# Rounding the cosine's multiple of 2π by an int32 output instead of by adding and taking off a large constant

## The chip, the cores and the metric

The kernel runs on one core of one Trainium2 chip. The metric is device microseconds (us) of one execution; the median of three runs of the kernel before is 973.51 us (972.93 to 973.61).

## The reference

The program is a linear attention followed by two feed-forward layers, all in float32. The change lies in the first feed-forward layer alone:

```python
def _moe_ref(x, w_in, w_out):
    h = x @ w_in            # 2304 tokens, 512 -> 2048
    g = h * np.cos(h)
    return (g @ w_out).astype(np.float32)

def _moe2_ref(x, w_in, w_out):
    h = x @ w_in
    r = np.maximum(h, 0.0)
    g = r * r
    return (g @ w_out).astype(np.float32)

x = _moe_ref(x=attention_output, ...)
return _moe2_ref(x=x, ...)
```

## The kernel before

**Stages.** The attention (lines 802 to 964) runs to about 190 us of the profiled execution, the first feed-forward layer from there to about 595 us, the second from there to the end. All products of the feed-forward layers are float32 results made of three matmuls each: every operand is split into a high part of reduced precision and the rest, and high·high, high·rest and rest·high are summed in PSUM.

**Blocks and chunks of the first layer.** `feed_forward` goes over five blocks of tokens (`BLOCKS`, line 290): blocks 0, 2, 3 and 4 have 512 tokens, block 1 has 256. In a block, step i (0 to 18) works on the 16 chunks of 128 hidden features. `G1` (line 308) multiplies the split input with the split weights of chunk i: 12 matmuls into one of four PSUM banks, `h`. `G2` (line 376) multiplies the finished g of chunk i−3 with the second weights: 12 matmuls into four accumulators. So TensorE is given G1 of chunk i and then G2 of chunk i−3 in each step; steps 16 to 18 hold G2 alone. The first matmul of a G2 needs the high part of g, the second already needs the rest of it.

**The elementwise chain of a chunk** is cut into seven parts in `part` (line 320), which stand in `elementwise` (line 350) in the order B1 of chunk i−1, A1 of chunk i, B2 of i−1, A2a of i, B3 of i−1, A2b of i, B4 of i−1. ScalarE (ACT) and VectorE (DVE) each do their own in that order:

- A1, ACT: line 329 writes h/2π plus 12582912 (1.5·2^23, so the addition rounds to a whole number) to t, line 330 takes the constant off again.
- A2a and A2b, DVE, lines 332 and 334: r = h − C1·t, then r = r − C2·t, with C1 + C2 = 2π.
- B1, ACT, lines 336 and 337: sin(r/2), then its square times 2.
- B2, DVE, line 339: t = (1 − r)·h, which is h·cos(h).
- B3, ACT, line 344: the high part of g. B4, DVE, line 347: the rest of g.

t and r are halves of a tile `tr` of which two exist; `h` has four banks, g two tiles.

**What stands between them.** In block 0 the weights of the first layer that are still missing are converted (`ticks`, with DVE doing the combining steps). In blocks 1 to 3 the weights of the second layer are prepared ahead (`ahead`, line 551, called by `converts`, line 744, at places fixed by a count of matmul columns): a load (line 474), two ACT steps (lines 239, 241), three DVE steps (260, 262, 269), one POOL step (264), POOL sums (504), and then pieces of the result are split (ACT line 524, DVE line 525) into staging areas and sent to DRAM by the SP queue (line 526). An ACT split has to wait until the DMA that last read its staging area has landed. Block 4 prepares nothing of this kind, only the last weights and the start of the second layer. SP issues its DMAs in program order.

The order of the first four chunks of block 0 is arranged together with the last attention units by a table of costs and places (`F_STEPS`, `arrange`); everything behind them is in the order in which the code is written.

Of the kernel before, what the change touches and what calls it, by code (L numbers as in the profile page):

```python
# [10 lines left out]
I32 = mybir.dt.int32  # L11
U32 = mybir.dt.uint32
ACTF = mybir.ActivationFunctionType
ALU = mybir.AluOpType
# [1 line left out]
PSUM = bass.MemoryType.PSUM  # L16

INV_2PI = 0.15915494309189535
ROUND = 12582912.0
C1 = 6.28125  # L20
C2 = 6.283185307179586 - C1
START_0 = 0
# [142 lines left out]
def attention_ffn_kernel(  # L165
# [11 lines left out]
    nc = tc.nc  # L177
# [12 lines left out]
    def f(t):  # L190
        return t.bitcast(F32)

    with tc.manual_schedule():
# [11 lines left out]
        def work(tag, shape, dtype=F32, name=None):  # L205

            return shared.tile(shape, dtype, tag=tag, name=name or tag, bufs=BUFS[tag])
# [15 lines left out]
        def w_load(n):  # L223
            part, c = order[n]
            s = w_slot(n + 1, I32, [P, KDM * P, 2], "raw")
            nc.sync.dma_start(
                out=s.rearrange("p f t -> p (f t)"), in_=(w_in1, w_out1)[part].bitcast(I32)[c * P:(c + 1) * P, :]
            )
            raw_t[0, n] = words_of(s.rearrange("p (a f) t -> p a (f t)", a=2))
# [43 lines left out]
        def w_split(layer, n, part):  # L273
            m = mag_t[layer, n]
            if part == 0:
                if layer == 0:
                    t = w_slot(n, F32R, [P, 2, KDM * P], "w")
                    weights[(0, *order[n])] = t
                else:
                    t = w_slot(12 + n[1], F32R, [P, 2, KDM * P], "w")  # L280
                    weights[1, 1, n[1]] = t
                nc.scalar.activation(out=t[:, 0], in_=m, func=ACTF.Copy)
            else:
                t = weights[(0, *order[n])] if layer == 0 else weights[1, 1, n[1]]
                engine = nc.gpsimd if layer == 0 and n < NEARLY - 1 else nc.vector
                engine.tensor_tensor(out=t[:, 1], in0=m, in1=f(t[:, 0]), op=ALU.subtract)
                mag_t.pop((layer, n))
# [6 lines left out]
        xs_t, h_t, g_t, tr_t, acc, early = {}, {}, {}, {}, [], set()  # L294

        def split_x(j, kk, part):
            _, o, n = BLOCKS[j]
            src = xbuf[:, kk, o:o + n]
            x = work(XS[kk][part], [P, n], F32R, "xs")
            if part == 0:  # L300
                nc.scalar.activation(out=x, in_=src, func=ACTF.Copy)
                xs_t[kk] = (x,)
            else:
                hi = xs_t[kk][0]
                nc.vector.tensor_tensor(out=x, in0=src, in1=f(hi), op=ALU.subtract)
                xs_t[kk] = (hi, x)
# [13 lines left out]
        def part(name, j, c):  # L320

            n = BLOCKS[j][2]
            if (name, j, c) in early:
                return
            if name == "A1":
                tr_t[c] = work("e", [P, 2, n], F32, "tr")
            t, r = tr_t[c][:, 0], tr_t[c][:, 1]
            if name == "A1":
                nc.scalar.activation(out=t, in_=h_t[c], func=ACTF.Copy, scale=INV_2PI, bias=ROUND)  # L329
                nc.scalar.activation(out=t, in_=t, func=ACTF.Copy, bias=-ROUND)  # L330
            elif name == "A2a":
                nc.vector.scalar_tensor_tensor(out=r, in0=t, scalar=-C1, in1=h_t[c], op0=ALU.mult, op1=ALU.add)  # L332
            elif name == "A2b":
                nc.vector.scalar_tensor_tensor(out=r, in0=t, scalar=-C2, in1=r, op0=ALU.mult, op1=ALU.add)  # L334
            elif name == "B1":
                nc.scalar.activation(out=r, in_=r, func=ACTF.Sin, scale=0.5)  # L336
                nc.scalar.activation(out=r, in_=r, func=ACTF.Square, scale=SQRT2)  # L337
            elif name == "B2":
                nc.vector.scalar_tensor_tensor(  # L339
                    out=t, in0=r, scalar=1.0, in1=h_t.pop(c), op0=ALU.subtract, op1=ALU.mult, reverse0=True  # L340
                )
            elif name == "B3":
                g_t[c] = g = work("kq1", [P, 2, n], F32R, "g")
                nc.scalar.activation(out=g[:, 0], in_=t, func=ACTF.Copy)  # L344
            else:
                g = g_t[c]
                nc.vector.tensor_tensor(out=g[:, 1], in0=t, in1=f(g[:, 0]), op=ALU.subtract)  # L347
                tr_t.pop(c)
# [781 lines left out]
```

## Time and profile before

| what | value |
|---|---|
| median of three runs | 973.51 us |
| profiled execution, its own time | 972.84 us |
| profiled execution, span | 971.1 us |
| TensorE matmul busy (PE) | 956.7 us, 99% |
| TensorE weight loads busy (PEld) | 823.8 us, 85% |
| VectorE busy | 662.6 us, 68% |
| ScalarE busy | 579.6 us, 60% |
| GpSimd busy | 168.8 us, 17% |
| granted TensorE clock, mean | 1.000 |

The span runs from the first instruction to the last; the execution's own time is 1.7 us longer. PE and PEld are two queues of the same engine: weight loads run beside the matmuls before them. The ends of matmuls are modelled, so PE's idle time is a lower bound for what the engine loses; a late weight load on PEld shows it more fully. An idle time is put down to what ended it.

### The profile page before, as it was taken

To read this page: it belongs to the slowest core of one execution; us is meant where nothing else is said; L and a number is where in the kernel's file an instruction comes from. 1 tells how busy PE (TensorE), PEld (TensorE's weight loads), DVE (VectorE), ACT (ScalarE), POOL (GpSimd) and SP (SyncE) were. 2 spreads that over 40 slices of the span, in tenths; PEclk is the share of its full clock that TensorE was granted. 3 is DMA by queue.
4 is the path that set the end of the run, shared out by engine and by line. 5 is a ranking of instruction groups with operands and counts; after the bars stand their busy time and mean duration, and the time that the engine had idled before them with its cause. 6 is when DMAs were issued, how large, how long until landed. Compare 5 with 4: busy or idle time off the path is not lost.

```text
span 971.1 us, 15675 instructions
## 1 busy us (share of the span) xinstructions
PE 956.7 (99%) x5865; PEld 823.8 (85%) x5865; DVE 662.6 (68%) x1137; ACT 579.6 (60%) x1133; POOL 168.8 (17%) x146
## 2 busy tenths in 40 slices
PE   8999999999999999999999999999999999999998
PEld 7888888788899887788788888889889898988887
DVE  6788897589957676775868656877673434844444
ACT  4988877688867667766867664455442223432233
POOL 1666764100002033113300001212000000000000
PEclk9999999999999999999999999999999999999999
DMA  7566542242021055325244315665554435544411
GB/s 255 169 209 221 182 149 69 67 168 77 1 88 44 24 181 176 98 77 197 110 149 136 102 34 178 192 201 188 184 165 128 127 105 191 163 130 129 111 43 65
DMA packets 52283, 128.27 MB, mean 132 GB/s; under 512 B 6384, under 2 KB 12144, under 8 KB 52208
## 3 DMA queue, kind: packets, MB, share of 16 engines
q1 hardware_dynamic: 52064, 127.21, 40.7%
q8 instruction: 46, 0.75, 0.3%
q14 instruction: 29, 0.24, 0.1%
q10 hardware_dynamic: 144, 0.07, 0.0%
HBM read 102.99 MB, written 24.19 MB: 131 GB/s over the span
## 4 chain that ended last, share of the span: by engine, by line
PE 52%; ACT 3%; DVE 2%; DMA 1%; issue 1%; POOL 0%; SPq 0%; ACTq 0%; DVEq 0%
PE acc L668 20%; PE m L613 18%; PE acc L387 8%; PE h L317 2%; PE h L316 2%; PE h L315 2%; DMA sp<-xbuf 1%; ACT tr L329 1%; DVE tr L332 0%; ACT tr L330 0%; DVE tr L334 0%; ACT tr L336 0%; ACT xbuf L524 0%; DVE g L347 0%; DVE xbuf L525 0%
## 5 line engine op out<-in xcount | busy, mean ns | idle before, releaser
L668 PE MATMUL acc<-w,g 128*128 128x512 f32 x864 | 226.0, 394 | 0.0
L387 PE MATMUL acc<-g,w 128*128 128x512 f32 (+1 forms) x960 | 212.2, 370 | 6.2 <-DVE g L347 5.9
L387 PEld LDWEIGHTS acc<-g,w 128*128 128x128 f32 x960 | 167.7, 188 | 40.7 <-DVE g L347 10.0
L668 PEld LDWEIGHTS acc<-w,g 128*128 128x128 f32 x864 | 159.7, 188 | 23.3
L613 PE MATMUL m<-xc,wc 128*128 128x384 f32 x864 | 173.7, 336 | 0.8 <-DVE t L636 0.8
L613 PEld LDWEIGHTS m<-xc,wc 128*128 128x128 f32 x864 | 154.5, 188 | 14.2 <-DVE t L636 1.3
L315 PE MATMUL h<-xs,w 128*128 128x512 f32 (+1 forms) x320 | 117.9, 369 | 0.0
L316 PE MATMUL h<-xs,w 128*128 128x512 f32 (+1 forms) x320 | 117.8, 368 | 0.0
L317 PE MATMUL h<-xs,w 128*128 128x512 f32 (+1 forms) x320 | 117.7, 368 | 0.0
L595 DVE TENSOR_TENSOR g<-t,g 128x384 fp32r<-128x384 f32 x96 | 53.6, 579 | 77.7 <-ACT g L594 77.6
L594 ACT ACTIVATE g<-t 128x384 fp32r<-128x384 f32 x96 | 47.3, 518 | 65.6 <-DVE t L627 65.3
L264 POOL TENSOR_TENSOR mag<-mag,raw 128x512 int32<-128x512 int32 x36 | 48.2, 1339 | 212.5 <-ACT tr L337 90.0
L332 DVE SCALAR_TENSOR_TENSOR tr<-tr,h 128x512 f32<-128x512 f32 (+1 forms) x80 | 50.7, 633 | 39.5 <-ACT tr L330 38.9
L339 DVE SCALAR_TENSOR_TENSOR tr<-tr,h 128x512 f32<-128x512 f32 (+1 forms) x80 | 50.5, 631 | 33.7 <-ACT tr L337 33.4
L315 PEld LDWEIGHTS h<-xs,w 128*128 128x128 f32 x320 | 60.3, 188 | 10.3 <-issue 0.2
L316 PEld LDWEIGHTS h<-xs,w 128*128 128x128 f32 x320 | 60.4, 189 | 10.0
L317 PEld LDWEIGHTS h<-xs,w 128*128 128x128 f32 x320 | 60.3, 189 | 9.9
L336 ACT ACTIVATE tr<-tr 128x512 f32<-128x512 f32 (+1 forms) x80 | 46.7, 584 | 31.5 <-DVE tr L334 30.9
L869 PEld LDWEIGHTS kv<-v,e 128*128 128x128 f32 x512 | 60.2, 192 | 3.2 <-issue 1.4
L869 PE MATMUL kv<-v,e 128*128 128x65 f32 x512 | 62.5, 275 | 0.2
L344 ACT ACTIVATE g<-tr 128x512 fp32r<-128x512 f32 (+1 forms) x80 | 46.3, 580 | 27.2 <-DVE tr L334 11.7
L850 DVE TENSOR_REDUCE m<-pj 128x4 f32<-128x512 f32 (+1 forms) x80 | 49.9, 623 | 18.0 <-PE pj L835 10.0
(93 smaller groups left out, 1393.5 us busy)
## 6 DMA issues: line engine op xcount, KB each, us to landing
wc<-sp SPq DMA_DIRECT2D x72, 512.0 KB
raw<-in_dram SPq DMA_DIRECT2D x48, 512.0 KB
xbuf<-in_dram SPq DMA_DIRECT2D x16, 512.0 KB
sp<-xbuf SPq DMA_DIRECT2D x15, 512.0 KB
kq<-in_dram SPq DMA_DIRECT2D x16, 384.0 KB
wc<-sp SPq DMA_DIRECT2D x24, 256.0 KB
v<-in_dram SPq DMA_DIRECT2D x16, 330.0 KB
dn<-db SPq DMA_DIRECT2D x32, 144.0 KB
```

What stands on the lines that cost most here:

```text
L264: soon(layer, n).tensor_tensor(out=halves(mi), in0=halves(mi), in1=word0, op=ALU.add)
L315: nc.tensor.matmul(out=hps, lhsT=ih[:, kk, :], rhs=xh, start=kk == 0, stop=False)
L316: nc.tensor.matmul(out=hps, lhsT=ih[:, kk, :], rhs=xl, start=False, stop=False)
L317: nc.tensor.matmul(out=hps, lhsT=il[:, kk, :], rhs=xh, start=False, stop=kk == KDM - 1)
L332: nc.vector.scalar_tensor_tensor(out=r, in0=t, scalar=-C1, in1=h_t[c], op0=ALU.mult, op1=ALU.add)
L339: nc.vector.scalar_tensor_tensor(out=t, in0=r, scalar=1.0, in1=h_t.pop(c), op0=ALU.subtract, op1=ALU.mult, reverse0=True)
L387: nc.tensor.matmul(out=acc[m][:, 0:n], lhsT=l, rhs=r, start=c == 0 and i == 0, stop=c == KFF - 1 and i == 2)
L595: nc.vector.tensor_tensor(out=g[:, 1], in0=t, in1=f(g[:, 0]), op=ALU.subtract)
L613: nc.tensor.matmul(out=m, lhsT=l[:, sl], rhs=r[:, q], start=start and q == 0 and n == 0, stop=q == 1 and n == 2, skip_group_check=True,)
L668: nc.tensor.matmul(out=acc[m], lhsT=g[:, l, sl], rhs=w[:, r], start=p == 0 and f_ == 0 and i == 0, stop=p == NP - 1 and f_ == 1 and i == 2,)
L850: nc.vector.tensor_reduce(out=m[:, 0:n], in_=pj[:, 0:n, :], axis=AX.X, op=ALU.max, apply_absolute_value=True)
L869: nc.tensor.matmul(out=acc[:, s, h, 0:D + 1], lhsT=e[:, t, s, :], rhs=v_t[u][:, t, h, 0:D + 1], start=t == 0 and h == 0 and s == 0, stop=F ...
```

## The change

In A1 the two activations become one. It multiplies h by 1/2π and writes the result as int32 into the words of t, so that the conversion rounds to a whole number; the addition of the large constant and the activation that takes it off (64 of 128x512 and 16 of 128x256 elements) are gone. A2a and A2b read t as int32 in place of float32. B2 writes t as float32 as before. No instruction stands at another place: on ACT 80 of 1036 rows of the program's order are left out, the order of the others and of all other engines is the same.

```diff
-ROUND = 12582912.0
...
             if name == "A1":
-                nc.scalar.activation(out=t, in_=h_t[c], func=ACTF.Copy, scale=INV_2PI, bias=ROUND)
-                nc.scalar.activation(out=t, in_=t, func=ACTF.Copy, bias=-ROUND)
+                nc.scalar.activation(out=t.bitcast(I32), in_=h_t[c], func=ACTF.Copy, scale=INV_2PI)
             elif name == "A2a":
-                nc.vector.scalar_tensor_tensor(out=r, in0=t, scalar=-C1, in1=h_t[c], op0=ALU.mult, op1=ALU.add)
+                nc.vector.scalar_tensor_tensor(out=r, in0=t.bitcast(I32), scalar=-C1, in1=h_t[c], op0=ALU.mult, op1=ALU.add)
             elif name == "A2b":
-                nc.vector.scalar_tensor_tensor(out=r, in0=t, scalar=-C2, in1=r, op0=ALU.mult, op1=ALU.add)
+                nc.vector.scalar_tensor_tensor(out=r, in0=t.bitcast(I32), scalar=-C2, in1=r, op0=ALU.mult, op1=ALU.add)
```

## Rows read from the trace of the kernel before

**Rows 1.** The page's busy times, and the span's stretch of block 0 (--windows view).

```profile
PE 956.7 (99%) x5865; PEld 823.8 (85%) x5865; DVE 662.6 (68%) x1137; ACT 579.6 (60%) x1133; POOL 168.8 (17%) x146
...
195.00:272.00 77.00, 77.00 (x341) 63.30 (x340) 71.56 (x124) 61.72 (x110) 2.88 (x2) 1.00 0.21 75
```

**Rows 2.** Groups by line and shape: busy us, mean ns, idle before and its releasers.

```profile
L387 PEld LDWEIGHTS acc<-g,w 128*128 128x128 f32 x960 | 167.7, 188 | 40.7 <-DVE g L347 10.0 <-ACT g L344 1.3
```

**Rows 3.** Waits of PEld in blocks 0, 1, 2, 3: us in total, times, longest.

```profile
PEld acc L387 <- DVE g L347: 0.6, 2, 0.3
...
PEld acc L387 <- DVE g L347: 1.8, 4, 0.7
...
PEld acc L387 <- DVE g L347: 5.5, 5, 1.3
...
PEld acc L387 <- DVE g L347: 2.2, 2, 1.3
```

**Rows 4.** Timeline of PEld in block 2, G2 of chunks 7 to 9: start, us.

```profile
368.88 0.19 PEld L387 LDWEIGHTS acc<-g,w 128*128 128x128 f32 x1
370.41 2.37 PEld L387 LDWEIGHTS acc<-g,w 128*128 128x128 f32 x11 [1.34 <-DVE g L347]
...
375.54 2.68 PEld L387 LDWEIGHTS acc<-g,w 128*128 128x128 f32 x12
...
380.98 2.68 PEld L387 LDWEIGHTS acc<-g,w 128*128 128x128 f32 x12
```

**Rows 5.** Timeline of ACT and DVE, block 3, one turn without preparation work.

```profile
418.41 0.63 ACT L336 ACTIVATE tr<-tr 128x512 f32<-128x512 f32 x1 [1.48 <-DVE tr L334]
...
419.62 0.58 ACT L329 ACTIVATE tr<-h 128x512 f32<-128x512 f32 x1
419.74 0.69 DVE L339 SCALAR_TENSOR_TENSOR tr<-tr,h 128x512 f32<-128x512 f32 x1 [1.36 <-ACT tr L337]
420.23 0.63 ACT L330 ACTIVATE tr<-tr 128x512 f32<-128x512 f32 x1
...
420.89 0.69 DVE L332 SCALAR_TENSOR_TENSOR tr<-tr,h 128x512 f32<-128x512 f32 x1 [0.46 <-ACT tr L330]
421.61 0.69 DVE L334 SCALAR_TENSOR_TENSOR tr<-tr 128x512 f32<-128x512 f32 x1
...
422.34 0.63 ACT L336 ACTIVATE tr<-tr 128x512 f32<-128x512 f32 x1 [0.96 <-DVE tr L334]
```

**Rows 6.** Groups by line and shape: the removed operation, and two with int32.

```profile
L330 ACT ACTIVATE tr<-tr 128x512 f32<-128x512 f32 x64 | 40.5, 632 | 2.0
...
L241 ACT ACTIVATE raw<-raw 128x512 int32<-128x512 uint32 x48 | 32.3, 673 | 1.0 <-DMA raw<-in_dram 1.0
...
L269 DVE SCALAR_TENSOR_TENSOR mag<-raw,mag 128x512 int32<-128x512 int32 x28 | 19.4, 692 | 1.0
...
L330 ACT ACTIVATE tr<-tr 128x256 f32<-128x256 f32 x16 | 6.7, 418 | 0.5
```

**Rows 7.** Timeline of block 3 around an ACT wait for a staging area.

```profile
429.14 0.66 ACT L239 ACTIVATE mag<-xbuf 128x512 f32<-128x512 f32 x1
...
432.48 1.31 POOL L264 TENSOR_TENSOR mag<-mag,xbuf 128x512 int32<-128x512 int32 x1 [16.21 <-ACT tr L329]
...
433.82 0.56 SPq L474 DMA_DIRECT2D xbuf<-in_dram  x1
...
434.46 1.06 SPq L526 DMA_DIRECT2D sp<-xbuf  x2
...
439.71 0.63 ACT L524 ACTIVATE xbuf<-xbuf 128x512 fp32r<-128x512 f32 x1 [5.52 <-DMA sp<-xbuf]
...
441.66 0.62 ACT L336 ACTIVATE tr<-tr 128x512 f32<-128x512 f32 x1
```

**Rows 8.** All waits of the span: us in total, times, longest.

```profile
ACT xbuf L524 <- DMA sp<-xbuf: 21.7, 4, 5.7
...
ACT tr L329 <- PE h L317: 14.6, 15, 2.3
```

## The prediction
> **What bounds the kernel now.** I read the busy times first: TensorE is at 99%, DVE at 68%, ACT at 60%, and in the stretch of block 0 the granted clock is 1.00, the upper of its two levels [rows 1]. So what an ACT step less can give is limited to the time in which TensorE waits for the chain that this step belongs to. The groups by line show that time: the weight loads of G2 stand idle 10.0 us for DVE's line 347, the rest of g, and 1.3 us for ACT's line 344, its high part [rows 2]. By blocks it is 0.6 us in block 0, 1.8 in block 1, 5.5 in block 2 and 2.2 in block 3; block 4, which prepares nothing, has none [rows 3].
>
> An idle weight load is not quite a late TensorE, since a load may run a little ahead of its matmul. In block 2, G2 of chunk 8 starts 6.66 us after G2 of chunk 7, and that of chunk 9 starts 5.44 us after that of chunk 8; between the first two lies an idle time of 1.34 us [rows 4]. So 1.34 us shown cost 1.22, nine tenths. Nine tenths of 11.3 us are 10.2; I use **10.0 us** as all that there is to gain.
>
> Why is line 347 late? One turn of the chain without preparation work takes 3.93 us, from line 336 at 418.41 to the next at 422.34, though in it DVE stands idle for 1.36 + 0.46 us and ACT for 0.96: they wait for one another [rows 5]. This is below the 5.44 us of a TensorE step, so the chain would keep up. But the preparation steps stand in the same two queues, and four times ACT waits 5 to 6 us for a staging area, 21.7 us in all [rows 8]. ACT is then far behind: only 15 of the 80 A1 steps wait for their matmuls [rows 8], in the others the matmuls were done before.
>
> **The change part by part.**
>
> *The activation removed.* It takes 632 ns at 512 columns and 418 at 256, with some 30 ns of idle time before it [rows 6]. Where ACT is what the chain goes through, 0.66 us go (0.45 in block 1). In the undisturbed turn less goes: line 332 starts at 420.89, just behind line 330, but without that step it must still wait for line 339, which ends at 419.74 + 0.69 = 420.43 [rows 5]. So it starts at about 420.46, **0.43 us** earlier, and the turn takes 3.50 us. DVE's line 339 is what is late next.
>
> Beside the row stands a rule. For an activation with constant scale and bias the Trainium skill (ScalarE: Activation LUTs, What ACT_TABLE_LOAD costs) states 186 ns plus 0.833 ns per element of a row, with 93 ns of overlap between neighbours: 520 ns for 512. By it the first chunk of a block would gain 0.52 in place of 0.66 us and my sum would come out about 0.15 us higher; I go by the row.
>
> *The int32 output.* No row shows a PSUM source with an int32 output. The nearest is line 241, which writes int32 in 673 ns, against 580 for line 329 [rows 5, 6]; so between nothing and 0.09 us more. I take nothing: in the undisturbed turn it lies beside line 339 anyway, with about 0.2 us of cover (line 329 ends at 420.20, line 339 at 420.43) [rows 5].
>
> *The int32 operand of lines 332 and 334.* Line 269 on the same engine, with the same operation form, reads two int32 tiles in 692 ns, though with bit operations; line 332 takes 690 with float32 [rows 5, 6]. I take nothing. The far end is the POOL row of an int32 addition of the same shape, 1.31 us [rows 7], 0.62 more for each; that makes a rival below.
>
> *What the removal does to each stall.* At the start of a block the gain is 0.66 us at chunk 0 and 0.43 more with each chunk, 1.95 at chunk 3. A wait for a staging area comes in between: does it keep its place? The DMA that ACT waits for at 439.71 was issued at 434.46, right behind a load (433.82) that waited for POOL's line 264 (432.48 to 433.79), whose input goes back to ACT's own line 239 at 429.14 [rows 7]. So the whole detour starts in the ACT queue and moves forward with it; only the turn that lies inside the detour saves nothing.
>
> - Block 3: the first stall costs under 0.9 us (2.2 less the longest, 1.3) [rows 3] and has 1.95 against it; both together, with the wait for line 344, cost about 2.1, with two more chunks by then, 2.8. Both go.
> - Block 2: at chunk 7 seven chunks have gained some 2.9 us (0.66, then 0.43 each, a little less where ACT reaches TensorE and has to wait for it) against 1.2. At chunk 10 it is 4.1 against 2.6 so far. At the end, where G2 follows G2 every 2.7 us, chunk 13 has 4.5 against 4.1, chunk 14 has 4.8 against 5.3. **0.5 us stay.**
> - Block 1: the first stall, under 0.7 us, has at least 0.45 against it; the three of the tail, 1.1 us, have a dozen chunks behind them. I leave 0.1.
> - Block 0: two stalls of 0.3 us at the tail; one chunk's 0.43 to 0.66 covers them.
>
> **The sum.** 10.0 − 0.6 = 9.4 us. Nothing else follows TensorE's clock or changes its matmuls. The profiled execution took 972.84 us, so 963.4 against it; it stands 0.67 us under the median 973.51, and against the median the forecast is **964.1 us**.
>
> **The rivals.**
>
> *The waits for the staging areas keep their place* (faster, but by half). If loads and spills land when the DMA queues let them and not when ACT asks, the four stalls that follow such a wait stay: twice 1.34 in block 2, 2.2 in block 3 [rows 3, 4], 4.7 us with nine tenths and the little that line 344 adds. 10.0 − 0.6 − 4.7 = 4.7 us, so 968.8. For it speaks the size of these waits, up to 5.7 us [rows 8]; against it the chain of rows 7, in which nothing before line 239 sets the date.
>
> *No change, 973.5.* Either the int32 output takes as long as both steps (0.58 + 0.63), against the row of line 241, or TensorE is bound by its own work. The Trainium skill (Perfetto Trace Analysis, Identifying the Most-Contended Engine) has one look for the engine with the highest occupancy, for TensorE by the weight loads' share, and better that one first; ACT's 60% against 85% would make this change worth nothing. The rows speak against it for this stretch: the 85% is a mean, and the idle loads name their cause.
>
> *DVE becomes the bound* (slower). If an int32 operand in arithmetic takes 0.62 us more on lines 332 and 334, DVE gets 16 × 1.24 = 19.8 us more in block 0, where it is busy 71.56 of 77.00 us already [rows 1]. 5.4 us are free, so TensorE waits 14 us there, more than all the gain of the other blocks; with no gain elsewhere it is 973.5 + 14 = 987.5. The point from which DVE decides is 5.4 / 32, about 0.17 us more for each of the two. Line 269 speaks against it.
>
> **How the numbers follow.** A measurement of this kernel can tell about 0.2%, 1.9 us, from no change. The forecast, with its own range 962.6 to 966, has a chance of 0.66; the staging rival, or something between, up to 969, has 0.20; no change 0.06; slower 0.05; and 0.03 that the start of the second layer or the whole 11.3 us shown come on top. The range takes the first two, 962.4 to 968.9, and leaves out 0.14. Faster 0.89, same 0.06, slower 0.05.
>
> **What the profile would show.** Right: line 330 is missing; line 332 waits for line 339 on its own engine and no longer for ACT; a clean turn takes 3.5 us; the idle time of G2's weight loads for DVE's line 347 falls from 10.0 us to about 0.5, left at the tail of block 2; lines 332 and 334 keep 0.69 us. The four waits for staging areas are still there, as long or longer, but earlier in the block. Wrong: the stalls behind these waits are still of 1 us (second case), or lines 332 and 334 have grown (slower case), or the new line of A1 takes over 0.8 us.

## The result, and the profile after

The changed kernel takes 963.0 us (median of five, 962.58 to 963.75) against 973.53 (median of five runs on the same chip). The ratio is 0.9893, 95% interval 0.9882 to 0.9904: between 9.3 and 11.5 us less, 10.5 by the medians. The forecast was 964.1 us, within 962.4 to 968.9.

On the page of the changed kernel, TensorE is still at 99%, and ACT has lost 42.7 us of busy time (579.6 in [rows 1]):

```profile
PE 953.5 (99%) x5865; PEld 824.9 (86%) x5865; DVE 657.4 (68%) x1137; ACT 536.9 (56%) x1053; POOL 169.0 (18%) x146
```

So of 42.7 us taken off ACT a quarter came back as time. The groups by line and shape answer to [rows 2, 6]; line numbers are lower by one or two than before (A1 is 328, A2a 330, A2b 332, B1 334 and 335, B2 337, B3 342, B4 345, G2 385):

```profile
L385 PEld LDWEIGHTS acc<-g,w 128*128 128x128 f32 x960 | 168.0, 189 | 30.5 <-DVE g L345 0.6
...
L332 DVE SCALAR_TENSOR_TENSOR tr<-tr 128x512 f32<-128x512 int32 x64 | 44.9, 701 | 1.9
...
L330 DVE SCALAR_TENSOR_TENSOR tr<-tr,h 128x512 f32<-128x512 int32 x64 | 43.6, 681 | 13.9 <-ACT tr L328 13.4
...
L328 ACT ACTIVATE tr<-h 128x512 int32<-128x512 f32 x64 | 37.5, 587 | 18.9 <-PE h L316 17.2 <-DVE g L345 1.5
```

The first row is the result: the weight loads of G2 wait 0.6 us for the rest of g where they waited 10.0, and no longer for its high part. The others show that the int32 form has no price of its own at 512 columns: 681 and 701 ns for the two DVE steps, 587 ns for A1. In the kernel before, with float32, they took 686, 704 and 585 ns:

```profile
L334 DVE SCALAR_TENSOR_TENSOR tr<-tr 128x512 f32<-128x512 f32 x64 | 45.0, 704 | 1.9
...
L332 DVE SCALAR_TENSOR_TENSOR tr<-tr,h 128x512 f32<-128x512 f32 x64 | 43.9, 686 | 32.9 <-ACT tr L330 32.4
...
L329 ACT ACTIVATE tr<-h 128x512 f32<-128x512 f32 x64 | 37.5, 585 | 15.3 <-PE h L317 13.8 <-DVE g L347 1.5
```

By stages, from the first weight load of G1 in each block to the next block's (and to the second layer's first product), in the profiled executions:

| us | block 0 | block 1 | block 2 | block 3 | block 4 | first product to end |
|---|---|---|---|---|---|---|
| before | 90.82 | 48.37 | 92.53 | 89.32 | 81.60 | 387.62 |
| after | 90.44 | 46.28 | 87.34 | 87.04 | 81.60 | 387.59 |
| difference | 0.38 | 2.09 | 5.19 | 2.28 | 0.00 | 0.03 |

Together 9.94 us. The span went down by less, 9.1 us (971.1 to 962.0), since block 0 began 0.84 us later in the second execution, at 181.65 against 180.81. That is no effect of the change: over the eleven profiled executions of this study it lies anywhere between 180.38 and 181.65.

The turn without preparation work, at the start of block 3 as in [rows 5] (timeline of ACT and DVE: start, us, then line and tile):

```profile
410.94 0.63 ACT L334 ACTIVATE tr<-tr 128x512 f32<-128x512 f32 x1 [1.48 <-DVE tr L332]
...
412.15 0.58 ACT L328 ACTIVATE tr<-h 128x512 int32<-128x512 f32 x1
412.27 0.69 DVE L337 SCALAR_TENSOR_TENSOR tr<-tr,h 128x512 f32<-128x512 f32 x1 [1.36 <-ACT tr L335]
412.88 0.68 DVE L330 SCALAR_TENSOR_TENSOR tr<-tr,h 128x512 f32<-128x512 int32 x1
413.00 0.63 ACT L342 ACTIVATE g<-tr 128x512 fp32r<-128x512 f32 x1 [0.26 <-DVE tr L337]
413.60 0.69 DVE L332 SCALAR_TENSOR_TENSOR tr<-tr 128x512 f32<-128x512 int32 x1
...
414.32 0.63 ACT L334 ACTIVATE tr<-tr 128x512 f32<-128x512 f32 x1 [0.69 <-DVE tr L332]
```

From line 334 to the next it is 3.38 us, 0.55 less than before. Line 330 has no idle time in front of it any more: it follows line 337 on its own engine.

The detour through a staging area in block 3, which answers to [rows 7]:

```profile
420.44 0.65 ACT L238 ACTIVATE mag<-xbuf 128x512 f32<-128x512 f32 x1
...
423.44 1.29 POOL L263 TENSOR_TENSOR mag<-mag,xbuf 128x512 int32<-128x512 int32 x1 [14.01 <-ACT tr L328]
...
424.76 0.57 SPq L472 DMA_DIRECT2D xbuf<-in_dram  x1
...
425.19 0.63 ACT L342 ACTIVATE g<-tr 128x512 fp32r<-128x512 f32 x1 [1.86 <-PE acc L385]
425.42 1.06 SPq L524 DMA_DIRECT2D sp<-xbuf  x2
425.72 0.62 ACT L522 ACTIVATE st<-xbuf 128x512 fp32r<-128x512 f32 x1
...
430.59 0.63 ACT L522 ACTIVATE xbuf<-xbuf 128x512 fp32r<-128x512 f32 x1 [4.25 <-DMA sp<-xbuf]
...
432.54 0.62 ACT L334 ACTIVATE tr<-tr 128x512 f32<-128x512 f32 x1
```

From the block's first A1 (408.87, before 415.67) to the B1 behind the detour (432.54, before 441.66) it is 23.7 us where it was 26.0: the detour came 2.3 us earlier in the block. The other three detours of blocks 2 and 3 end 2.3, 3.3 and 3.4 us earlier in their blocks. In all waits of the span (us, times, longest) two rows of the kernel after tell the rest:

```profile
ACT g L342 <- PE acc L385: 46.7, 32, 2.1
...
ACT xbuf L522 <- DMA sp<-xbuf: 19.4, 4, 5.2
```

The four waits for a staging area are still there, 19.4 us of the 21.7 in [rows 8]. But ACT now waits 46.7 us for TensorE to free a tile of g: the chain runs ahead, and TensorE sets its pace. In the kernel before that wait was short:

```profile
ACT g L344 <- PE acc L387: 5.0, 5, 1.4
```

### The profile page after: what moved, and what is told of

Read it like the earlier page. It is cut to its first block, busy times and chain, and to the rows that moved or that the text cites. A ratio compares the mean times of both kernels' runs of the same rounds, so it can differ in the third digit from the quotient of the medians.

```text
span 962.0 us, 15555 instructions
## 1 busy us (share of the span) xinstructions
PE 953.5 (99%) x5865; PEld 824.9 (86%) x5865; DVE 657.4 (68%) x1137; ACT 536.9 (56%) x1053; POOL 169.0 (18%) x146
## 4 chain that ended last, share of the span: by engine, by line
PE 94%; DMA 2%; ACT 2%; DVE 1%; POOL 0%; SPq 0%; issue 0%; DVEq 0%; ACTq 0%; POOLq 0%
PE acc L385 21%; PE acc L666 20%; PE m L611 18%; PE h L314 7%; PE h L315 7%; PE h L316 7%; PE kv L867 5%; PE nm L913 3%; PE pj L833 2%; PE nm L921 2%; PE tp L890 1%; PE kv L875 1%; PE pj L842 1%; DMA raw<-in_dram 1%; ACT eq L901 1%; ACT e L859 0%
## 5 line engine op out<-in xcount | busy, mean ns | idle before, releaser
L385 PE MATMUL acc<-g,w 128*128 128x512 f32 (+1 forms) x960 | 208.6, 368 | 0.0
L342 ACT ACTIVATE g<-tr 128x512 fp32r<-128x512 f32 (+1 forms) x80 | 47.0, 589 | 69.2 <-PE acc L385 46.7
L337 DVE SCALAR_TENSOR_TENSOR tr<-tr,h 128x512 f32<-128x512 f32 (+1 forms) x80 | 50.5, 631 | 35.5 <-ACT tr L335 35.2
L345 DVE TENSOR_TENSOR g<-tr,g 128x512 fp32r<-128x512 f32 (+1 forms) x80 | 52.8, 660 | 24.7 <-ACT g L342 24.7
L330 DVE SCALAR_TENSOR_TENSOR tr<-tr,h 128x512 f32<-128x512 int32 (+1 forms) x80 | 50.2, 628 | 16.0 <-ACT tr L328 15.5
```

The lines of the kernel that those rows point to most:

```text
L330: nc.vector.scalar_tensor_tensor(out=r, in0=t.bitcast(I32), scalar=-C1, in1=h_t[c], op0=ALU.mult, op1=ALU.add)
L337: nc.vector.scalar_tensor_tensor(out=t, in0=r, scalar=1.0, in1=h_t.pop(c), op0=ALU.subtract, op1=ALU.mult, reverse0=True)
L385: nc.tensor.matmul(out=acc[m][:, 0:n], lhsT=l, rhs=r, start=c == 0 and i == 0, stop=c == KFF - 1 and i == 2)
```

## The experiments

The theory: the gain is the shorter turn of the chain, which lets ACT and DVE get ahead before each detour; the detours then fall into a lead and TensorE does not see them. Rivals: the int32 form itself pays; ACT's occupancy is what counts, whatever step is taken off; the waits for the staging areas alone make the stalls. The kernel before ran beside each group of runs: 973.62 us in the first (e1 to e4), 973.35 in the second (e5 to e7), 973.46 in the third (e8, e9).

**The chain as long as before, with the int32 form.**

```diff
                 nc.scalar.activation(out=t.bitcast(I32), in_=h_t[c], func=ACTF.Copy, scale=INV_2PI)
+                nc.scalar.activation(out=t.bitcast(I32), in_=t.bitcast(I32), func=ACTF.Copy)
```

> The changed kernel with one more ACT step behind A1 that copies t onto itself (int32 to int32, the same shape), so that A2a again waits for two ACT steps in a row. If the gain comes from the shorter chain, it goes back to the time before: 973.5 us, 972.5 to 974.5, with some 10 us of idle weight loads of G2. If the int32 form itself (conversion, operands, the missing constant) were what pays, it stays near 963 to 965.

Measured: 973.8 us (973.07 to 974.78), ratio 1.0005 (0.9996 to 1.0013). The whole gain is lost. The added step takes 633 ns, as the removed one did (632). Its waits (B4 is line 346, G2 line 386):

```profile
ACT xbuf L523 <- DMA sp<-xbuf: 22.6, 4, 5.9
...
PEld acc L386 <- DVE g L346: 10.8, 13, 1.3
```

The 10 us of idle weight loads are back too, in 13 waits, as many as in [rows 3]. With the chain as long as before, the int32 form costs and pays nothing that can be told from noise.

**A step beside the chain, but with the chain's input.**

```diff
+        junk = const.tile([P, 512], mybir.dt.bfloat16, tag="junk", name="junk")
...
                 nc.scalar.activation(out=t.bitcast(I32), in_=h_t[c], func=ACTF.Copy, scale=INV_2PI)
+                nc.scalar.activation(out=junk[:, 0:n], in_=h_t[c], func=ACTF.Copy, scale=INV_2PI)
```

> The changed kernel with one more ACT step behind A1 that writes h, scaled, as bf16 to a tile nobody reads: ACT is as busy as before, but A2a does not wait for the step. If the chain is what counts, the clean turn stays at 3.5 us (ACT's steps in it sum to some 3.1) and most of the gain stays: 963.5 to 966 us. If ACT's occupancy is what counts, all of it goes back: 972 to 974 us.

Measured: 967.69 us (967.63 to 968.84), ratio 0.9944 (0.9931 to 0.9956): between the two theories, and outside both expected ranges. The timeline of the clean turn says why this run does not separate them (A1 is line 329, the added step 330, A2a 332, B1 336):

```profile
415.37 0.63 ACT L336 ACTIVATE tr<-tr 128x512 f32<-128x512 f32 x1 [1.48 <-DVE tr L334]
...
416.57 0.58 ACT L329 ACTIVATE tr<-h 128x512 int32<-128x512 f32 x1
...
417.05 0.59 ACT L330 ACTIVATE junk<-h 128x512 bf16<-128x512 f32 x1
...
417.67 0.69 DVE L332 SCALAR_TENSOR_TENSOR tr<-tr,h 128x512 f32<-128x512 int32 x1 [0.28 <-ACT junk L330]
...
419.12 0.64 ACT L336 ACTIVATE tr<-tr 128x512 f32<-128x512 f32 x1 [0.96 <-DVE tr L334]
```

A2a starts when the added step has ended (417.64), though the only tile that the two share is h, which both read: the expectation's "A2a does not wait for the step" failed. The turn is 3.75 us, and the gain 5.9 us: turns of 3.93, 3.75 and 3.38 us go with 0, 5.9 and 10.5 us.

**The same, with a tile of its own.** The step copies a bf16 tile onto itself, at the same place.

```diff
+        junk = const.tile([P, 512], mybir.dt.bfloat16, tag="junk", name="junk")
+        nc.vector.memset(junk, 0.0)
...
                 nc.scalar.activation(out=t.bitcast(I32), in_=h_t[c], func=ACTF.Copy, scale=INV_2PI)
+                nc.scalar.activation(out=junk[:, 0:n], in_=junk[:, 0:n], func=ACTF.Copy)
```

> The changed kernel with one more ACT step behind A1 that copies a bf16 tile of its own onto itself (128x512, or 128x256 in block 1), at the place of the step that the change removed. It shares no tile with the chain, so A2a waits for A1 alone (in e2_beside A2a waited for the added step too, and the clean turn was 3.75 us). If the chain's length is what counts, the clean turn is 3.5 us and most of the gain stays: 963.3 to 966 us. If ACT's occupancy counts as much, 968 to 973 us.

Measured: 963.51 us (962.49 to 964.6), ratio 0.9898 (0.9884 to 0.9911). ACT has as many steps as in the kernel before, of 0.62 us each, and the gain stays. In its clean turn (A1 line 330, added step 331, A2a 333, B3 345, B1 337) A2a no longer waits for the step, and B3 follows it with little delay:

```profile
409.70 0.63 ACT L337 ACTIVATE tr<-tr 128x512 f32<-128x512 f32 x1 [0.96 <-DVE tr L335]
...
410.90 0.58 ACT L330 ACTIVATE tr<-h 128x512 int32<-128x512 f32 x1
...
411.37 0.62 ACT L331 ACTIVATE junk<-junk 128x512 bf16<-128x512 bf16 x1
411.63 0.68 DVE L333 SCALAR_TENSOR_TENSOR tr<-tr,h 128x512 f32<-128x512 int32 x1
411.89 0.62 ACT L345 ACTIVATE g<-tr 128x512 fp32r<-128x512 f32 x1
...
413.07 0.63 ACT L337 ACTIVATE tr<-tr 128x512 f32<-128x512 f32 x1 [0.56 <-DVE tr L335]
```

The turn is 3.37 us. That settles latency against occupancy at this place.

**The same step, ahead of B1.**

```diff
+                nc.scalar.activation(out=junk[:, 0:n], in_=junk[:, 0:n], func=ACTF.Copy)
                 nc.scalar.activation(out=r, in_=r, func=ACTF.Sin, scale=0.5)
```

> The changed kernel with the same step of its own tile, but ahead of B1, where ACT stands idle in a clean turn (0.69 us before line 334) because it waits for A2b. There it costs the chain least: 963 to 965 us if the chain counts; 968 to 973 us if occupancy does. It can be worse than e8_free only in turns with preparation steps, where ACT does not wait at that place.

Measured: 967.52 us (966.61 to 968.1), ratio 0.9936 (0.9922 to 0.995). This is 2.5 us above the first expected range and just below the second. In a clean turn the step does lie in ACT's idle time: the first turn of block 3 stays at 3.37 us. In a turn with preparation work it does not (added step line 336, A2b 334, B1 337, the preparation's split 525):

```profile
420.08 0.92 ACT L525 ACTIVATE xbuf<-mag 128x512 fp32r<-128x512 f32 x2
420.14 0.69 DVE L334 SCALAR_TENSOR_TENSOR tr<-tr 128x512 f32<-128x512 int32 x1
...
420.91 0.61 ACT L336 ACTIVATE junk<-junk 128x512 bf16<-128x512 bf16 x1
421.43 0.62 ACT L337 ACTIVATE tr<-tr 128x512 f32<-128x512 f32 x1
```

A2b has ended at 420.83, but ACT comes from the preparation at 421.00 and does the added step first: B1 starts at 421.43. So behind preparation steps ACT's queue itself is the chain, and there a step costs. From B1 to B1 this turn takes 3.94 us; the same turn of block 3 takes 3.93 in the kernel before, 3.42 in the changed kernel and 3.54 with the step behind A1. In that place the step stands ahead of B3, for which ACT waits for DVE even in turns with preparation work (0.39 us at 419.89 in the changed kernel). Blocks 1 to 3 are 46.43, 90.48 and 87.67 us long: most of the loss is in block 2, 3.1 us.

**One block at a time.** `ti` is t as int32 in the blocks listed in `INT_IN`, in the others the old two steps stand.

```diff
+INT_IN = (2,)
...
-                nc.scalar.activation(out=t.bitcast(I32), in_=h_t[c], func=ACTF.Copy, scale=INV_2PI)
+                if j in INT_IN:
+                    nc.scalar.activation(out=t.bitcast(I32), in_=h_t[c], func=ACTF.Copy, scale=INV_2PI)
+                else:
+                    nc.scalar.activation(out=t, in_=h_t[c], func=ACTF.Copy, scale=INV_2PI, bias=ROUND)
+                    nc.scalar.activation(out=t, in_=t, func=ACTF.Copy, bias=-ROUND)
```

> The change in block 2 alone, the old two steps in the others. By the stalls per block as the two traces show them (block 2 is 5.2 us shorter): 968.3 us, 967.5 to 969. If block 2's gain needed what the earlier blocks gain, or if the blocks share one cause that moves from one to the next (a stall gone here comes back in block 3), 970 to 972.

Measured: 967.71 us (967.44 to 969.69), ratio 0.9945 (0.9932 to 0.9959), 5.9 us less and within the expected range. In its profile block 2 takes 87.20 us, block 3 89.71, blocks 0 and 1 90.99 and 48.43.

> The change in blocks 0 and 1 alone. By the traces these are 0.4 and 2.1 us shorter: 971.0 us, 970.3 to 971.8. If the sum of the blocks is not additive, or the start of block 2 inherits the lead, less than 970.

The second run has `INT_IN = (0, 1)`. Measured: 970.55 us (970.15 to 972.32), ratio 0.9972 (0.9962 to 0.9983), 3.1 us less, also within the expected range. Blocks 0 and 1 take 90.44 and 46.31 us, block 2 92.77, block 3 89.45. Block 2, and blocks 0 and 1 together, have their own gain, about as large as in the full change, and a stall that goes does not come back in the next block. Block 3 was not changed alone.

**The staging waits, in the kernel before.**

```diff
-AHEAD_FIRST, AHEAD_NEXT, AHEAD_STAGE, AHEAD_LOAD = 14.0, 8.6, 7.0, 9.5
+AHEAD_FIRST, AHEAD_NEXT, AHEAD_STAGE, AHEAD_LOAD = 14.0, 8.6, 7.0, 8.0
```

> The kernel before (two steps in A1) with the loads of the preparation 1.5 counts later (AHEAD_LOAD 8.0 in place of 9.5), which puts each load behind the sends of the staging areas on SP's queue, so that a send no longer waits for the POOL step that the load waits for. If the stalls of blocks 2 and 3 need both the slow turn and the long waits for a staging area, the waits (21.7 us) shrink to less than half and up to 4.7 us go: 968.5 to 971 us. If the slow turn alone makes the stalls, nothing moves: 973 to 974 us. Against it: a later load may make ACT wait at line 239 instead.

Measured: 966.47 us (965.47 to 967.02), ratio 0.9925 (0.9911 to 0.9938), 6.9 us less, where up to 4.7 were expected. In its waits there is none of ACT for a sent staging area any more; in their place (all waits, line numbers as before):

```profile
ACT xbuf L524 <- POOL mag L264: 8.4, 2, 4.2
...
ACT mag L239 <- DMA xbuf<-in_dram: 6.5, 2, 3.3
...
PEld acc L387 <- DVE g L347: 3.7, 8, 1.0
```

The first two rows sum to 14.9 us in place of 21.7: they did not fall below half, as had been expected, and yet more of the stalls went. The second row is the wait at line 239 that the expectation names. Blocks 2 and 3 take 88.09 and 87.05 us: 4.4 and 2.3 us less, with the old turn of A1. So the stalls there need both, the slow turn and the late send; taking away either does nearly all. Block 1, which has no such wait, keeps its 48.41 us.

> The changed kernel with the same move of the loads. Only some 0.3 us of stalls are left in blocks 1 and 2, so it stays at 962.7 to 963.3 us by either theory, unless the later loads are waited for: then 964 or more.

The same line in the changed kernel. Measured: 962.63 us (962.18 to 963.77), ratio to the kernel before 0.9891 (0.9877 to 0.9904). It is the lowest median of the study, 0.07 us under the expected range, but the spread of its runs covers that of the changed kernel. In its profile block 2 takes 86.96 in place of 87.34 us; the next run, whose edit acts only from block 4 on, has 87.73 there, so this difference is scatter as far as these profiles tell.

**The largest stall that is left.**

```diff
-LATE_AT = (-1, 1, 3, *range(5, 44, 3))
+LATE_AT = (-1, 1, 3, 6, *range(8, 44, 3))
```

> The changed kernel with the fourth late tile of the second layer's weights one step later (LATE_AT 6 in place of 5), so that its three DVE steps no longer stand ahead of line 634, for which TensorE waits 1.0 us at the head of the second layer, the largest stall that is left. If these DVE steps are the cause: 962.0 us, 961.7 to 962.4. If line 634 is late for another reason, or the stall moves on a step: 963.0 us.

Measured: 963.76 us (963.61 to 964.26), ratio to the kernel before 0.9901 (0.9888 to 0.9915): no gain, and 0.8 us above the second case. The waits of PEld from 560 to 700 us, which were 1.3 us for line 634 and 0.4 us for line 655 in the changed kernel, are now:

```profile
PEld m L611 <- ACT t L655: 0.9, 2, 0.5
PEld m L611 <- ACT t L628: 0.7, 1, 0.7
PEld m L611 <- DVE t L634: 0.3, 1, 0.3
```

The wait for line 634 falls from 1.3 to 0.3 us, so the DVE steps did hold it; but the stall moved on to ACT, as the second case said: the three rows sum to 1.9 us.

## Why the prediction was right

**What there is to gain** was put at 10.0 us, nine tenths of the idle weight loads. Blocks 0 to 3 got 9.94 us shorter where 9.4 were forecast, and 0.6 us of idle loads are left: right, and a little too small. Block 1 shows it best: 2.09 us, where nine tenths of the 1.8 us of [rows 3], less 0.1, make 1.5. The 0.5 us by which the blocks got shorter than forecast are half of the distance between the forecast of 964.1 us and the measured 963.0; the other half is within the scatter of the medians.

**The undisturbed turn** was put 0.43 us shorter; it is 0.55, 3.38 us. The mechanism, that DVE's B2 takes over, is what the timeline shows; the size was off because I let A2a begin when B2's row ends. It begins 0.08 us before (412.88 against 412.96). The first chunk gained what the row of line 330 said: its B1 stands 5.23 us behind the start of block 3, and 5.89 before, 0.66 less.

**The lead in block 2** was built from these turns and came out too large all the same. B1 of chunks 7 and 10 comes 2.35 and 3.35 us earlier in the block, not 2.9 and 4.1: some turns with preparation work save next to nothing. From chunk 2 to 3 it is 6.07 us after 6.11, as ACT now waits 1.97 us for DVE ahead of B3 where it waited 1.33; from 3 to 4 it is 5.89 both times, as it now waits 1.50 us for another staging area where it waited 1.25. The text let nearly every chunk save. So a turn that was put too long and too many turns counted offset each other in part, which is luck. The conclusion holds since the lead is still above the 1.2 and 2.6 us that it has to cover. Block 2 got 5.19 us shorter where 4.8 were forecast (5.3 less the 0.5 that stay), block 3 2.28 where it was 2.1. What stays is where it was expected, two waits of 0.3 us at the tail of block 2.

**The detours move forward with ACT's queue**: shown, by 2.3 to 3.4 us for all four. In block 3 B1 of chunk 3, ahead of the first detour, comes 1.88 us earlier, against 1.95 in the text; B1 of chunk 4, behind it, 2.30, so the turn with the detour saved 0.42 us where the text has nothing. The rival in which the waits keep their place is out. That they would be "as long or longer" was wrong: 19.4 us after 21.7. In the detour of [rows 7] the send went out at 425.42, 0.9 us before ACT was done with the split ahead (425.72 + 0.62); before, it went out 0.3 us after (434.46 against 433.57 + 0.62). ACT came later to its wait because it had stood 1.86 us for TensorE ahead of line 342 (425.19): part of the lead turns into waiting for TensorE.

**int32 costs nothing**: right on all three lines, and the slower rival with it. e1 shows it apart from the rest.

**Against the rule of the most-contended engine** (the Trainium skill, Perfetto Trace Analysis, Identifying the Most-Contended Engine): it has one find the engine with the highest occupancy and optimize that one first. ACT at 60% was not that engine, and a step taken off it was worth 1.1% all the same. So the reading that the prediction's no-change rival made of the rule, that a step on another engine is worth nothing, does not hold here. e8 shows the other half: the same occupancy put back where the chain does not pass left 963.51 us.

What the medians show beyond the blocks, 10.5 against 9.9 us, is within the scatter of the start of block 0, and 9.9 lies inside the interval too; I don't claim it.

## What to carry to other kernels

When two engines hand a tile back and forth, work out the turn: which end releases which start, all the way round; a step is worth what it adds to the turn, not its duration, and the engine's occupancy tells neither. A stall on the bound engine can need two causes at once (a slow turn and a late send here); either may be the cheap one to remove, and their gains do not add. Put extra work where the queue waits anyway in its busiest turns, not where it waits in the clean ones.

## What the runs showed that was not expected

- A step on ACT that reads the same PSUM tile as the DVE step behind it held that DVE step back until it had ended (417.64, start 417.67), though neither writes it. A2a starts 0.03 to 0.06 us behind the end of this step in 61 of the 80 chunks and in no chunk before it; where the step has a tile of its own (e8) it starts before the step's end in 63. The trace shows that the program orders them: in that run A1 updates a semaphore in 2 of 80 chunks and the added step in all, so A2a waits for the added step's signal; in e8 A1 signals by itself in all 80. Whether the two reads could run side by side was not tried.
- One line that moves the loads behind the sends on SP's queue gave 6.9 of the 10.5 us without touching the computation; together with the change it gave nothing that can be told from noise.
- The same added ACT step cost 4.5 us ahead of B1 (967.52 against 963.0) but only 0.5 us, within the scatter, behind A1 (963.51). In the profiles of the latter, blocks 0 to 3 are as long as in the changed kernel, to within 0.04 us each.
